# Capping the bytes of loads in flight at 1.25 MB in a two-layer decode kernel

## The chip, the cores and the metric

The kernel runs on one core of a Trainium2 chip. Its time is device time in microseconds (us), and lower is better. Runs of one kernel spread by about 1%; a run more than 1.5% above the fastest of its kernel counts as slow and is left out of the ratios (the medians quoted are of all runs). A ratio is the mean time of one kernel's fast runs over that of the other's of the same rounds on the same chip, so it is not quite the ratio of the medians quoted beside it.

The engines: TensorE (PE; its weight loads are PEld), VectorE (DVE), ScalarE (ACT), and SyncE (SP), which issues all DMA loads.

## The reference, cut to what matters

```python
def setup_inputs():                        # bfloat16 throughout
    x: (4, 1, 448)                         # 4 sequences ("tokens" below), one position each
    k_cache, v_cache: (4, 8, 8192, 256)    # 8 KV heads, 16 query heads
    wq: (448, 4096); wo: (4096, 448); w_gate, w_up: (448, 1792); w_down: (1792, 448)

x = x + A(layernorm(x))     # attention over the last 2048 positions of the cache
x = x + B(layernorm(x))     # FFN: (silu(x @ w_gate) * (x @ w_up)) @ w_down
x = x + A(layernorm(x))     # layer 2: the same weights and the same caches
x = x + B(layernorm(x))
```

There are 4 tokens x 8 heads x 2 layers = 64 "pairs" of one token with one KV head. A pair needs 1 MB of K and 1 MB of V; 16 pairs of the second layer find theirs still in SBUF. Everything loaded is 112.85 MB. (Sizes of loads and caps count 1 MB as 2^20 bytes, so 1.25 MB is 1.31 million bytes; totals, bytes in flight as measured, and rates count in millions.)

## The kernel before

The kernel builds a graph of operations, runs its own list scheduler over it, and emits each engine's instructions in the order planned, with the semaphore waits that the dependencies need. SyncE is an engine in this plan too: a load may be planned as soon as its destination is free, and nothing limits how many are queued.

```python
def dma(self, rank, nbytes, emit, sem, r=(), w=()):
    o = self.op(SP, 0.05, rank, emit, r=r, w=w)
    ...
def schedule(self):
    rate = 400e3
    ...
        t, e = best                      # earliest engine that has something ready
        o = min((o for o in avail[e] if ready_at[o] <= t + 1e-9), key=lambda o: (o.rank, o.i))
        o.start = t
        free[e] = t + o.dur
        if o.nbytes:
            chan = max(chan, t + 0.6) + o.nbytes / rate
            o.end = chan + 1.3           # planned landing
...
NK = 2; NKT = 5; NV = 6                  # buffers: raw K, transposed K, V
load(kvh + 0.6, 458752, wo_sb[...], ...)             # output projection, a piece per head
load(7.2, 3 * 458752, wg_sb[...], ...)               # FFN weights, whole
load(7.3, 1605632, wd_sb[...], ...)
...
for pos, (t, layer, kvh) in enumerate(seq):          # 64 pairs
    # K: two loads of 512 KB into a raw buffer; VectorE transposes each half (line KT)
    # V: four loads of 256 KB
    # TensorE: S = scores, M = maximum, P and Y = probabilities times V, A = output projection
```

A load is planned when its buffer is free. The weights' buffers are free from the start, so the plan puts V for six pairs, as many as there are buffers, and all output-projection and FFN loads ahead of the third pair's K, whose raw buffer waits for a transpose.

## Time and profile before

| | before |
|---|---|
| time, median (range) | 408.95 us (406.32 to 409.17, 3 runs) |
| TensorE, VectorE busy | 63%, 50% of the span |
| loads: share of 16 engines, mean rate | 76.6%, 280 GB/s |
| first FFN starts; second q projection starts | 109.3 us; 122.6 us |

From the page of the kernel before: busy tenths and the rate of the loads in 40 slices of 10.2 us each, the load queue's share, the chain that ended last, and the loads (count, KB each, median us from issue to landing):

```profile
PE   2155006638647656688778575887874778578965
...
DMA  7999999987970899973974999939849949745300
GB/s 304 386 387 382 399 396 398 395 269 232 397 266 14 265 392 395 396 270 116 378 278 152 385 399 395 354 110 336 300 161 322 395 157 340 259 142 185 101 2 3
...
q1 hardware_dynamic: 49184, 112.85, 76.6%
...
PE 40%; DVE 17%; DMA 15%; SPq 13%; issue 10%; ACT 4%; DVEq 0%
DMA Kr<-in_A_k_cache_dram 15%; DVE KT L528 11%; PE S L544 9%; PE Y L592 8%; SPq L536 7%; PE Z L437 6%; SPq L312 5%; PE A L611 5%; PE Z L399 3%; PE Z L456 3%; ACT oT L601 2%; DVE negm L560 1%; ACT qb L421 1%; PE Z L342 1%; PE Z L344 1%
...
Kr<-in_A_k_cache_dram SPq DMA_DIRECT2D x96, 512.0 KB, 7.6
V<-in_A_v_cache_dram SPq DMA_DIRECT2D x192, 256.0 KB, 8.1
```

In slices 2 to 8 the loads run at 382 to 399 GB/s, yet TensorE is busy at most six tenths of a slice and not at all in slices 5 and 6: it is starved although the load queue is full, because the wrong things are loaded. Later the loads pause again and again (14, 116, 110 GB/s). A load lands some 8 us after its issue: there is a long queue in front of it. (Z is the tile of the q projection and the FFN; the names of lines and tiles are the kernel's.)

SyncE's timeline of the kernel before (start, length, line and tiles, count), and TensorE's longest waits there (total us, times, longest):

```profile
35.96 2.77 SPq L312 DMA_DIRECT2D wg_sb<-in_B_w_gate_dram  x2
38.78 2.79 SPq L312 DMA_DIRECT2D wu_sb<-in_B_w_up_dram  x2
41.62 0.43 SPq L312 DMA_DIRECT2D wd_sb<-in_B_w_down_dram  x1
42.09 9.07 SPq L312 DMA_DIRECT2D wo_sb<-in_A_wo_dram  x1
51.21 2.84 SPq L522 DMA_DIRECT2D Kr<-in_A_k_cache_dram  x4
```

```profile
PE S L544 <- DVE KT L528: 31.8, 9, 22.4
...
PE S L565 <- DVE negm L560: 17.9, 9, 6.6
...
PE S L544 <- issue: 11.2, 9, 2.2
PE Y L592 <- issue: 9.2, 6, 2.7
PE Z L456 <- issue: 6.3, 4, 2.6
```

The third pair's K is issued at 51.2 us, behind all the weights. TensorE waits 22.4 us for its transpose. "Issue" is time in which TensorE waited for nothing that the profile shows; summed over its lines it is 36 us. The trace holds 60 transfers of 16,384 bytes on a queue called instruction, and all 17 "issue" waits of 1 us or more begin between 0.3 us before and 1.4 us after the start of one of them. So I call these waits instruction waits below; the name is a reading of that coincidence.

### The profile page before, as it was taken

The page shows a single profiled execution, that of the slowest core. Times are in us where ns is not written, and L with a number is a line of the kernel's source. Part 1 is how long each engine was busy: PE and PEld are TensorE (multiplying, and loading weights), DVE is VectorE, ACT ScalarE, POOL GpSimd, SP SyncE. Part 2 cuts the span into 40 slices and gives each one's busy share as a digit, 9 for nine tenths or more (in the row PEclk, how much of TensorE's full clock was granted, in tenths as well). Part 3 has the DMA queues.
Part 4 walks back from the last instruction along what each step waited for, and adds up shares of the span by engine and source line. Part 5 has one row for each costly group of instructions (what it writes and reads, how often), then busy time and mean ns, then how long its engine had stood idle before and what let it go on. Part 6 is the DMA issues. An engine that isn't in the chain of part 4 may idle for free.

```text
span 406.4 us, 16676 instructions
## 1 busy us (share of the span) xinstructions
PE 254.8 (63%) x7572; PEld 230.5 (57%) x7572; DVE 203.1 (50%) x642; ACT 58.6 (14%) x302; POOL 2.7 (1%) x11
## 2 busy tenths in 40 slices
PE   2155006638647656688778575887874778578965
PEld 2154005537646645577677465776763768467854
DVE  6721026668523554556537554746355365546432
ACT  1014001102101111111112111110121211011210
POOL 2000000000000000000000000000000000000000
DMA  7999999987970899973974999939849949745300
GB/s 304 386 387 382 399 396 398 395 269 232 397 266 14 265 392 395 396 270 116 378 278 152 385 399 395 354 110 336 300 161 322 395 157 340 259 142 185 101 2 3
DMA packets 49255, 113.91 MB, mean 280 GB/s; under 512 B 4889, under 2 KB 11041, under 8 KB 48801
## 3 DMA queue, kind: packets, MB, share of 16 engines
q1 hardware_dynamic: 49184, 112.85, 76.6%
q8 instruction: 60, 0.98, 1.0%
q14 instruction: 11, 0.08, 0.1%
HBM read 112.82 MB, written 0.00 MB: 278 GB/s over the span
## 4 chain that ended last, share of the span: by engine, by line
PE 40%; DVE 17%; DMA 15%; SPq 13%; issue 10%; ACT 4%; DVEq 0%
DMA Kr<-in_A_k_cache_dram 15%; DVE KT L528 11%; PE S L544 9%; PE Y L592 8%; SPq L536 7%; PE Z L437 6%; SPq L312 5%; PE A L611 5%; PE Z L399 3%; PE Z L456 3%; ACT oT L601 2%; DVE negm L560 1%; ACT qb L421 1%; PE Z L342 1%; PE Z L344 1%
## 5 line engine op out<-in xcount | busy, mean ns | idle before, releaser
L528 DVE STREAM_TRANSPOSE KT<-Kr 128x1024 uint32<-128x1024 uint32 x96 | 118.3, 1235 | 50.2 <-DMA Kr<-in_A_k_cache_dram 50.1
L544 PE MATMUL S<-qb,KT 128*128 128x8 bf16 x2048 | 65.0, 168 | 49.7 <-DVE KT L528 31.8
L544 PEld LDWEIGHTS S<-qb,KT 128*128 128x128 bf16 x2048 | 61.0, 105 | 53.6 <-DVE KT L528 33.3
L592 PE MATMUL Y<-pT,V 128*128 128x2 bf16 x2048 | 63.9, 165 | 14.3 <-issue 9.2
L592 PEld LDWEIGHTS Y<-pT,V 128*128 128x128 bf16 x2048 | 59.8, 104 | 16.5 <-issue 9.8
L611 PE MATMUL A<-oT,wo_sb 128*128 128x1 bf16 x1024 | 37.4, 166 | 17.6 <-ACT oT L601 12.5
L611 PEld LDWEIGHTS A<-oT,wo_sb 128*128 128x128 bf16 x1024 | 32.9, 105 | 25.4 <-ACT oT L601 19.5
L601 ACT ACTIVATE oT<-Y,rinv 128x2 bf16<-128x2 f32 x128 | 26.5, 258 | 112.9 <-PE S L565 50.9
L550 DVE TENSOR_REDUCE pmax<-S 128x2 bf16<-128x32 f32 x64 | 11.8, 184 | 48.2 <-PE S L544 46.4
L560 DVE TENSOR_REDUCE negm<-M 128x2 bf16<-128x256 f32 x64 | 26.1, 407 | 12.3 <-PE M L557 11.3
L569 ACT ACTIVATE praw<-S 128x32 bf16<-128x32 f32 x64 | 12.6, 196 | 99.8 <-PE S L565 99.8
L437 PE MATMUL Z<-xn,wu_sb 128*128 128x1 bf16 x336 | 24.1, 165 | 2.0 <-issue 2.0
L437 PE MATMUL Z<-xn,wg_sb 128*128 128x1 bf16 x336 | 24.1, 165 | 1.4 <-DVE xe L381 1.4
L565 PE MATMUL S<-negm,identb 128*128 128x32 bf16 x64 | 12.3, 192 | 19.5 <-DVE negm L560 17.9
L581 DVE TENSOR_REDUCE rs<-Y 128x2 f32<-128x32 f32 x64 | 11.3, 178 | 19.3 <-PE P L576 13.6
L557 PE MATMUL M<-identb,pmax 128*128 128x128 bf16 x64 | 20.1, 314 | 0.0
L437 PE MATMUL Z<-xe,wu_sb 128*128 128x1 bf16 x112 | 18.5, 165 | 1.7 <-issue 1.7
L565 PEld LDWEIGHTS S<-negm,identb 128*128 128x128 bf16 x64 | 6.9, 108 | 21.7 <-DVE negm L560 21.5
L437 PE MATMUL Z<-xe,wg_sb 128*128 128x1 bf16 x112 | 18.5, 165 | 1.1 <-issue 1.1
L437 PEld LDWEIGHTS Z<-xn,wu_sb 128*128 128x128 bf16 x336 | 17.7, 104 | 2.2 <-issue 2.1
L437 PEld LDWEIGHTS Z<-xn,wg_sb 128*128 128x128 bf16 x336 | 17.6, 104 | 1.8 <-DVE xe L381 1.8
L555 PE MATMUL M<-identb,pmax 128*128 128x128 bf16 x64 | 17.4, 272 | 1.8 <-DVE pmax L550 1.8
(70 smaller groups left out, 313.0 us busy)
## 6 DMA issues: line engine op xcount, KB each, us to landing
Kr<-in_A_k_cache_dram SPq DMA_DIRECT2D x96, 512.0 KB, 7.6
V<-in_A_v_cache_dram SPq DMA_DIRECT2D x192, 256.0 KB, 8.1
wo_sb<-in_A_wo_dram SPq DMA_DIRECT2D x8, 448.0 KB, 9.5
wq_sb<-in_A_wq_dram SPq DMA_DIRECT2D x3, 1024.0 KB, 6.9
wd_sb<-in_B_w_down_dram SPq DMA_DIRECT2D x1, 1568.0 KB, 14.6
wg_sb<-in_B_w_gate_dram SPq DMA_DIRECT2D x1, 1344.0 KB, 11.5
wu_sb<-in_B_w_up_dram SPq DMA_DIRECT2D x1, 1344.0 KB, 12.6
wq_sb<-in_A_wq_dram SPq DMA_DIRECT2D x1, 512.0 KB, 9.7
```

The lines of the kernel that those rows point to most:

```text
L312: return e.dma_start(dst, src)
L437: last = e.matmul(Zb[:, 32 * gi + fc:32 * gi + fc + 1], lhsT=lhsT, rhs=rhs, start=(n == 0), stop=(n == 111), skip_group_check=True)
L528: return e.transpose(dst[:, 2 * hf:2 * hf + 2], src[:, 2 * hf:2 * hf + 2])
L536: g.dma(pos + 0.3, 1 << 18, lambda e, vs=vs, vsrc=vsrc, a=a: e.dma_start(Vs[vs][:, a, :, :], vsrc[:, a, :, :]), f"v{vs}_{a}", w=(f"v{vs}_{ ...
L544: last = e.matmul(Sb[p_][:, 8 * gg:8 * gg + 8], lhsT=kt[:, gg, ce // 2, ce % 2, :], rhs=qb[t][:, kvh, ce, :, :], start=(gg == 0 and ce == ...
L555: e.matmul(Mb[:, 0:128], lhsT=pmax[p_][:, 0:1].broadcast_to([128, 128]), rhs=identb[:, :], start=True, stop=False, skip_group_check=True)
L557: return e.matmul(Mb[:, 128:256], lhsT=pmax[p_][:, 1:2].broadcast_to([128, 128]), rhs=identb[:, :], start=False, stop=True, skip_group_che ...
L560: g.op(DVE, 0.4, pos, lambda e, p_=p_: e.tensor_reduce(negm[p_][:, :], Mb[:, 0:256].rearrange("p (n k) -> p n k", n=2), AX.X, ALU.max, neg ...
L565: return e.matmul(Sb[p_][:, 0:32], lhsT=identb[:, :], rhs=negm[p_][:, :].unsqueeze(1).broadcast_to([128, 16, 2]), start=False, stop=True, ...
L592: last = e.matmul(Yb[p_][:, 2 * dh:2 * dh + 2], lhsT=Vs[vs][:, a, gg, 128 * dh:128 * dh + 128], rhs=pT[p_][:, k, :], start=False, stop=(dh ...
L601: last = e.activation(oT[p_][:, n, :], Yb[p_][:, 0:4].rearrange("p (d n) -> p n d", n=2)[:, n, :], ACT.Copy, scale=rinv[p_][:, n:n + 1])
L611: last = e.matmul(Ab[:, 4 * t + cc:4 * t + cc + 1], lhsT=wo_sb[:, 4 * kvh + k, c0:c0 + 128], rhs=oT[p_][:, k // 2, k % 2:k % 2 + 1], start ...
```

## The change

Its intent: issue loads in the order of need, and never queue much more than the memory needs to stay busy. SyncE waits, before each load, for the landing of an earlier one such that at most 1.25 MB (5 x 256 KB) is in flight, the new load included. The plan knows it, so the planned order shifts as well. The FFN weights are cut into pieces that fit.

```diff
+INFLIGHT = 5 << 18
...
+    @staticmethod
+    def _gate(issued, o):
+        if o.rank < 0:
+            return None
+        total = o.nbytes
+        for d in reversed(issued):
+            total += d.nbytes
+            if total > INFLIGHT:
+                return d
+        return None
...
             avail[e].remove(o)
+            if o.nbytes:
+                o.gate = self._gate(order[SP], o)
+                if o.gate is not None:
+                    t = max(t, o.gate.end)          # in the plan
             o.start = t
...
-            for d in sorted(o.deps, key=lambda d: -d.end):
-                if o.deps[d] and not has(k, d):
+            deps = dict(o.deps)
+            if o.nbytes and o.gate is not None:
+                deps[o.gate] = True                 # the wait itself
+            for d in sorted(deps, key=lambda d: -d.end):
+                if deps[d] and not has(k, d):
...
-            load(7.2, 3 * 458752, wsb[:, 0:3 * FF]..., nm + "a")
+            for cc in range(3):
+                load(7.2, 458752, wsb[:, cc * FF:cc * FF + FF], src[128 * cc:128 * cc + 128, :], f"{nm}{cc}")
...
-        load(7.3, 1605632, wd_sb[:, :, :], ..., "wd")
+        for i, k0 in enumerate((0, 4, 8, 12)):
+            k1 = min(k0 + 4, NFC)
+            load(7.3, (k1 - k0) * 114688, wd_sb[:, k0:k1, :], wd_v[:, k0:k1, :], f"wd{i}")
```

So there are three parts: a new order, the waits (the cap), and the pieces.

More of the change, by code (lines that the diff above doesn't have):

```diff
@@ L40 @@
     __slots__ = ("i", "eng", "dur", "rank", "emit", "deps", "succ", "nbytes", "dsem", "dval",
-                 "start", "end", "pos", "waits", "inc", "val", "known")
+                 "start", "end", "pos", "waits", "inc", "val", "known", "gate")
     def __init__(self, i, eng, dur, rank, emit):
@@ L323, in build @@
         for nm, wsb, src in (("wg", wg_sb, B_w_gate), ("wu", wu_sb, B_w_up)):
-            load(7.2, 3 * 458752, wsb[:, 0:3 * FF].rearrange("p (c n) -> p c n", c=3),
-                 src[0:384, :].rearrange("(c p) n -> p c n", p=128), nm + "a")
-            load(7.2, 229376, wsb[:, 3 * FF:], src[384:448, :].rearrange("r (h n) -> (r h) n", h=2), nm + "b")
-        load(7.3, 1605632, wd_sb[:, :, :], B_w_down.rearrange("(k p) n -> p k n", p=128), "wd")
+            for cc in range(3):
+                load(7.2, 458752, wsb[:, cc * FF:cc * FF + FF], src[128 * cc:128 * cc + 128, :], f"{nm}{cc}")
+            load(7.2, 229376, wsb[:, 3 * FF:], src[384:448, :].rearrange("r (h n) -> (r h) n", h=2), nm + "3")
+        wd_v = B_w_down.rearrange("(k p) n -> p k n", p=128)
+        for i, k0 in enumerate((0, 4, 8, 12)):
+            k1 = min(k0 + 4, NFC)
+            load(7.3, (k1 - k0) * 114688, wd_sb[:, k0:k1, :], wd_v[:, k0:k1, :], f"wd{i}")
         def small(t, rank, emit, r, w, dur=0.14, bank=()):
@@ L440, in gu @@
                 return last
-            g.op(PE, 3.4, rank, gu, r=(f"xn{t}", f"xe{t}", "wga", "wgb", "wua", "wub"), w=("z",), bank=("Z",))
+            g.op(PE, 3.4, rank, gu, r=(f"xn{t}", f"xe{t}", *(f"{n}{c}" for n in ("wg", "wu") for c in range(4))), w=("z",), bank=("Z",))
             g.op(SCA, 0.25, rank, lambda e: e.activation(th[:, :], Zb[:, 0:NFC], ACT.Tanh, scale=0.5), r=("z",), w=("th",),
@@ L459, in down @@
                 return last
-            g.op(PE, 1.8, rank, down, r=("hT", "wd"), w=("z",), bank=("Z",))
+            g.op(PE, 1.8, rank, down, r=("hT", "wd0", "wd1", "wd2", "wd3"), w=("z",), bank=("Z",))
             small(t, rank, lambda e: e.tensor_tensor(xs[:, t, 0, :], xs[:, t, 0, :], Zb[:, 64:68], op=ALU.add),
```

## The prediction

> **What bounds it now.** Not one engine. The page gives TensorE 63% of 406.4 us, VectorE 50%, the load queue 77%. The chain of waits: TensorE 40%, VectorE 17%, the K loads 15%, SyncE's issuing 13%, "issue" (TensorE waiting for nothing shown) 10%. By stages (windows): from 10 to 80 us the loads run at 382 to 399 GB/s while TensorE idles. SyncE's timeline shows why: after the first two K pairs it issues every V, output-projection and FFN weight load, and the third pair's K only at 51.2 us; its data land at 58.7. TensorE waits 22.4 us there for the transpose. FFN 1 starts at 109.3 us, the second q projection at 122.6. Afterwards a period of 16 pairs takes 83 to 87 us and moves some 25 MB (63 us at 397 GB/s); loads stand idle around each q projection (2 GB/s from 120 to 130 us) because buffers are full.
>
> **Removed.**
> 1. The wrong load order. The order listing of the changed kernel has K before V, pair by pair, FFN weights just before pair 7's V. TensorE follows the stream from about 20 us on. FFN 1 needs fewer S groups ahead of it (10 instead of 12).
> 2. Instruction starvation. TensorE's waits named "issue" sum to 36 us (27 waits, up to 2.7 us). The trace has 60 instruction transfers of 16 KB (the Trainium skill, "Runtime: NRT & Kernel Launch", Terms, gives 16 KiB refills). Stalls of 1.4 to 2.7 us fall where 7 to 14 loads are in flight, under 0.8 mostly where 3 or fewer are. The skill's "DMA: Bandwidth & Descriptors", Queues, rings and completion order, says rings are served in turn per packet, which would make depth harmless; the trace suggests otherwise. I expect about half of it back.
>
> **Added.** A waiting SyncE. A lone 512 KB K load takes 3.56 us from issue to landing, a lone 256 KB V 2.75; at 0.66 us per 256 KB that leaves a fixed 2.1 us. With 1.25 MB in flight I work out 5.8 us per fresh pair (2 MB) instead of 5.3; 7.4 with an output-projection piece instead of 6.4; the FFN weights, two 448 KB pieces in flight, 17 us instead of 12. [...]
>
> **On the critical path.** Start: FFN 1 near 98 us, second q projection 112 to 118 instead of 122.6: minus 5 to 10. Later periods: TensorE gains 4 to 5 us of issue stalls each and 3 to 5 us from K no longer queued behind V bursts (7.75 us K landings at 136.7 and 99.4). Against that, 12 fresh pairs at 5.8 us plus some 1 us of instruction hits each are about 80 us, close to the period itself, so the loads become a second, nearly equal limit and part of the gain is lost in imperfect overlap.
>
> Predicted 399 us, range 378 to 425. Chances: faster by over 2% 0.50, within 2% 0.28, slower 0.22.
>
> **What would show it.** K third pair landing near 25 us, not 58.7; the 22.4 us TensorE wait gone; median K landing 3.5 to 4.5 us instead of 7.6; GB/s of 300 to 350 in the first 90 us instead of 395; "issue" on TensorE at 12 to 22 us instead of 36; SyncE waiting mostly for loads; less full idleness of the queue at q projections.
>
> **What would make it wrong.** If instruction transfers halt the shallow stream for 2 us or more each, or the fixed latency under load is nearer 2.6 us, loads run below 300 GB/s and bound everything: 420 to 435 us. If the issue stalls vanish altogether and buffers hide the slower stream, 375 to 385.

## The result, and the profile after

The changed kernel takes 461.49 us (460.91 to 462.42, 4 runs) against 407.63 us (4 runs): ratio 1.132, 95% interval 1.126 to 1.138. It is clearly slower, far outside the predicted range.

The same parts of the page for the changed kernel (slices of 11.5 us):

```profile
PE   2243532401456735638757835557677487667874
...
DMA  7987877878786987887778777887797787877300
GB/s 313 333 245 274 258 262 239 261 229 259 261 285 221 280 281 258 282 263 250 250 257 267 258 255 259 261 282 243 273 292 265 264 282 239 297 267 235 117 3 2
...
q1 hardware_dynamic: 49296, 112.85, 74.3%
...
DMA 68%; PE 18%; DVE 7%; issue 3%; ACT 2%; SPq 1%; DVEq 0%
DMA V<-in_A_v_cache_dram 32%; DMA Kr<-in_A_k_cache_dram 25%; DMA wo_sb<-in_A_wo_dram 7%; PE S L568 4%; PE Y L616 4%; DVE KT L552 4%; PE A L635 2%; DMA wu_sb<-in_B_w_up_dram 2%; PE Z L461 2%; PE Z L423 2%; PE Z L480 1%; ACT oT L625 1%; DMA wg_sb<-in_B_w_gate_dram 1%; DMA wd_sb<-in_B_w_down_dram 1%; ACT qb L445 1%
...
Kr<-in_A_k_cache_dram SPq DMA_DIRECT2D x96, 512.0 KB, 5.1
V<-in_A_v_cache_dram SPq DMA_DIRECT2D x192, 256.0 KB, 4.2
```

The pauses are gone, and so is the rate: from the third slice to the 37th it is 221 to 297 GB/s, never 390. The same bytes are moved by engines that are busy 74.3% of a longer span. DMA makes up 68% of the chain that ended last; it was 15% before. A K load lands 5.1 us and a V load 4.2 us after its issue, instead of 7.6 and 8.1, but so few are in flight that this caps the rate.

SyncE's waits in the changed kernel, and TensorE's:

```profile
SPq L560 <- DMA Kr<-in_A_k_cache_dram: 129.6, 80, 10.3
SPq L546 <- DMA V<-in_A_v_cache_dram: 54.3, 57, 2.4
...
SPq L208 <- DMA V<-in_A_v_cache_dram: 26.0, 32, 2.7
```

```profile
PE Y L616 <- DMA V<-in_A_v_cache_dram: 37.7, 8, 19.9
PE S L589 <- DVE negm L584: 28.2, 14, 7.1
...
PE S L568 <- DVE KT L552: 17.6, 4, 5.7
PE Y L616 <- issue: 16.3, 8, 4.2
```

SyncE now waits for the loads themselves. (L546 issues K, L560 V; L208 is the line that emits waits.) The order did what it was meant to: SyncE's timeline has the third pair's K issued at 21.0 us, and the 22.4 us wait for a transpose is gone. But TensorE waits 19.9 us once for the V behind the FFN weights.

```profile
15.55 2.90 SPq L560 DMA_DIRECT2D V<-in_A_v_cache_dram  x4
18.93 0.38 SPq L333 DMA_DIRECT2D wo_sb<-in_A_wo_dram  x1
21.00 2.79 SPq L546 DMA_DIRECT2D Kr<-in_A_k_cache_dram  x2
23.84 5.59 SPq L560 DMA_DIRECT2D V<-in_A_v_cache_dram  x4
```

Reading the latency against the window: from 15 us on, the trace has 1.19 MB in flight on average, and a load (weighted by bytes) lands after 4.62 us. 1.19 MB / 4.62 us = 258 GB/s, the measured rate, as it must be: the three figures are bound to each other by arithmetic, so this is no evidence of a cause. The question is where the 4.6 us come from, and whether order or waits cost the time.

### The profile page after: what moved, and what is told of

Its sections match the earlier page's. It is cut to its first block, busy times and chain, and to the rows that moved or that the text cites. A ratio compares the mean times of both kernels' runs of the same rounds, so it can differ in the third digit from the quotient of the medians.

```text
span 459.1 us, 16738 instructions
## 1 busy us (share of the span) xinstructions
PE 254.4 (55%) x7572; PEld 229.8 (50%) x7572; DVE 204.0 (44%) x642; ACT 59.0 (13%) x302; POOL 2.7 (1%) x11
## 3 DMA queue, kind: packets, MB, share of 16 engines
q1 hardware_dynamic: 49296, 112.85, 74.3%
## 4 chain that ended last, share of the span: by engine, by line
DMA 68%; PE 18%; DVE 7%; issue 3%; ACT 2%; SPq 1%; DVEq 0%
DMA V<-in_A_v_cache_dram 32%; DMA Kr<-in_A_k_cache_dram 25%; DMA wo_sb<-in_A_wo_dram 7%; PE S L568 4%; PE Y L616 4%; DVE KT L552 4%; PE A L635 2%; DMA wu_sb<-in_B_w_up_dram 2%; PE Z L461 2%; PE Z L423 2%; PE Z L480 1%; ACT oT L625 1%; DMA wg_sb<-in_B_w_gate_dram 1%; DMA wd_sb<-in_B_w_down_dram 1%; ACT qb L445 1%
## 5 line engine op out<-in xcount | busy, mean ns | idle before, releaser
L568 PE MATMUL S<-qb,KT 128*128 128x8 bf16 x2048 | 63.9, 168 | 34.3 <-DVE KT L552 17.6
L635 PEld LDWEIGHTS A<-oT,wo_sb 128*128 128x128 bf16 x1024 | 33.9, 106 | 19.8 <-ACT oT L625 19.1
L574 DVE TENSOR_REDUCE pmax<-S 128x2 bf16<-128x32 f32 x64 | 11.6, 182 | 45.2 <-PE S L568 45.1
L593 ACT ACTIVATE praw<-S 128x32 bf16<-128x32 f32 x64 | 12.6, 197 | 83.0 <-PE S L589 82.8
L423 PE MATMUL Z<-xn,wq_sb 128*128 128x1 bf16 (+1 forms) x480 | 17.7, 165 | 1.3 <-DVE xe L405 1.3
```

Source lines behind the costliest of these rows:

```text
L423: last = e.matmul(o, lhsT=lhsT, rhs=rhs, start=(hh == 0 and ee == 0 and cc == 0), stop=(hh == 15 and ee == 1 and cc == 3), skip_group_chec ...
L568: last = e.matmul(Sb[p_][:, 8 * gg:8 * gg + 8], lhsT=kt[:, gg, ce // 2, ce % 2, :], rhs=qb[t][:, kvh, ce, :, :], start=(gg == 0 and ce == ...
L593: g.op(SCA, 0.35, pos, lambda e, p_=p_: e.activation(praw[p_][:, :], Sb[p_][:, 0:32], ACT.Exp, scale=1.0 / 16.0), r=(f"s{p_}",), w=(f"praw ...
L635: last = e.matmul(Ab[:, 4 * t + cc:4 * t + cc + 1], lhsT=wo_sb[:, 4 * kvh + k, c0:c0 + 128], rhs=oT[p_][:, k // 2, k % 2:k % 2 + 1], start ...
```

## The experiments

All variants below are the changed kernel with the constant split in two, so that plan and waits can be capped separately:

```diff
-INFLIGHT = 5 << 18
+SCHED_INFLIGHT = 5 << 18     # what the plan, and so the order, assumes; None: no cap
+WAIT_INFLIGHT = 10 << 18     # what SyncE really waits for; None: no waits
-    def _gate(issued, o):
-        if o.rank < 0:
+    def _gate(issued, o, limit):
+        if limit is None or o.rank < 0:
...
-                o.gate = self._gate(order[SP], o)
-                if o.gate is not None:
-                    t = max(t, o.gate.end)
+                g = self._gate(order[SP], o, SCHED_INFLIGHT)
+                if g is not None:
+                    t = max(t, g.end)
+                o.gate = self._gate(order[SP], o, WAIT_INFLIGHT)
```

With the plan's value at 5 << 18, all instructions stand in the changed kernel's order on every engine; with None they stand in the order of before, save for the FFN pieces. The waits are not needed for correctness, so leaving them out is free of races.

Theory A: the waits cap the rate, because a load takes some 4.5 us to land. Theory B: the new order itself makes the loads slow.

### Order alone, waits alone, pieces alone, and 2.5 MB

The order alone: `WAIT_INFLIGHT = None`.

> The changed kernel's instruction order on every engine, none of its waits for earlier loads. Theory A (the waits cap the loads: with several loads in flight one takes some 4.5 us to land, and 1.25 MB in 4.5 us is no more than 290 GB/s): loads back at 390 GB/s in the busy stretches, time 380 to 405 us, that is at or below before. Theory B (the new order itself makes the loads slow): 435 to 460 us with 250 to 300 GB/s.

Measured: 399.92 us (4 runs), ratio 0.976 (0.969 to 0.984). Faster, though the interval does not clear 2%. I read the profile of its repeat, `new_order_free_b` below; its rate is back at 373 to 403 GB/s in slices 2 to 10:

```profile
GB/s 301 384 399 390 399 390 403 386 397 373 256 304 256 399 398 378 235 186 319 194 162 327 395 398 379 165 220 352 262 159 375 316 184 360 197 156 192 91 2 3
```

The waits alone: `SCHED_INFLIGHT = None`, `WAIT_INFLIGHT = 5 << 18`.

> The order of before (with the FFN weights in pieces), and each load held back to 1.25 MB in flight. Theory A: loads at 240 to 270 GB/s through the first 100 us and in every later busy stretch, 450 to 480 us. Theory B: near before, 405 to 425 us.

Measured: 473.50 us, ratio 1.160 (1.152 to 1.168). The old order at the same cap has the changed kernel's low rate:

```profile
GB/s 320 331 301 281 239 243 249 249 262 234 227 252 240 178 256 236 267 251 267 225 247 255 247 250 256 268 287 246 248 272 250 238 269 243 240 277 250 143 3 1
```

The pieces alone: both None.

> Only the FFN weights in 448 KB pieces, no waits, the order of before. Both theories: within 1% of before (404 to 412 us). If the pieces alone cost, over 415 us.

Measured: 408.33 us, ratio 1.002 (0.997 to 1.007). The pieces cost nothing.

The new order with twice the window: `WAIT_INFLIGHT = 10 << 18`.

> The changed kernel's order with 2.5 MB in flight instead of 1.25. Theory A: latency grows to some 6.5 us by the queue alone, the loads run at 350 to 390 GB/s, time 385 to 415 us. Theory B: no change, 435 to 460 us. A third theory (a fixed cost of each wait of SyncE, whatever the depth): 440 to 460 us as well, since the number of waits is much the same.

Measured: 393.94 us, ratio 0.965 (0.958 to 0.971). Faster than before. Theory A holds in all four runs; B fails in the three where it forecast something else (for the pieces both said the same); the third theory, a fixed cost of each wait, falls too: this program waits for landings about as often (258 such waits in its listing against 247 in the changed kernel's), and the loss is gone. The rate of this run, and its K and V landings:

```profile
GB/s 305 383 399 391 397 387 401 386 396 399 307 283 288 400 368 358 267 234 335 170 174 350 396 393 398 181 250 307 204 214 369 277 224 392 177 138 176 83 2 2
...
Kr<-in_A_k_cache_dram SPq DMA_DIRECT2D x96, 512.0 KB, 6.5
V<-in_A_v_cache_dram SPq DMA_DIRECT2D x192, 256.0 KB, 6.2
```

It runs at 383 to 401 GB/s through slices 2 to 10, with landings of 6.5 and 6.2 us.

### How deep must it be, and do coarse loads waste the window

`WAIT_INFLIGHT = 7 << 18`:

> The changed kernel's order with 1.75 MB in flight. If the rate is simply the bytes in flight over the landing time (1.19 MB over 4.6 us is the 258 GB/s of the changed kernel; at 1.7 MB I expect some 5.2 us), the loads run at about 325 GB/s and the time is 405 to 425 us. If there is a threshold and not a slope, it is within 1% of 2.5 MB (390 to 398 us) or of 1.25 MB (456 to 466 us).

Measured: 427.67 us, ratio 1.041 (1.033 to 1.049). A slope, not a threshold, and a little worse than I expected: from 15 us on the profiled run has 1.57 MB in flight and 5.57 us per load, so 281 GB/s over the stretch (which also contains pauses).

`WAIT_INFLIGHT = 14 << 18`:

> The changed kernel's order with 3.5 MB in flight. If 2.5 MB is already enough to keep the loads at their full rate and a deeper queue only lengthens TensorE's waits for instructions (42 us at 2.5 MB, 52 us with no cap), 394 to 400 us, with instruction waits between those two. If 2.5 MB still costs rate, 385 to 392 us.

Measured: 398.84 us, ratio 0.972 (0.966 to 0.979). TensorE's instruction waits were 44.7 us in the profiled run. The interval overlaps that of 2.5 MB: above 2.5 MB no further gain was seen.

K in loads of 256 KB at 1.25 MB (each transpose now waits for two of them, a line left out here):

```diff
-                for hf in range(2):
+                for qq in range(4):
...
-                        return e.dma_start(Kr[kr][:, 2048 * hf:2048 * hf + 2048], ...)
-                    g.dma(pos - 1.2, 1 << 19, kload, f"k{kr}_{hf}", w=(f"kr{kr}_{hf}",))
+                        return e.dma_start(Kr[kr][:, 1024 * qq:1024 * qq + 1024], ...)
+                    g.dma(pos - 1.2, 1 << 18, kload, f"k{kr}_{qq}", w=(f"kr{kr}_{qq}",))
```

> The changed kernel at 1.25 MB with each 512 KB K load cut into two of 256 KB, so that five equal loads can be in flight. If coarse pieces waste the window (the mean in flight is 1.19 MB of 1.31), it fills and a load lands sooner: 425 to 450 us. If only the bytes in flight count and these were nearly full already: 450 to 465 us.

Measured: 447.79 us, ratio 1.091 (1.086 to 1.097). Finer loads take back about a third of the loss (1.132 to 1.091) but no more.

The changed kernel with its one constant at 2.5 MB, `INFLIGHT = 10 << 18`:

> The changed kernel with its one constant at 2.5 MB, in the scheduler's plan too, so that the order shifts a little. If the plan's order matters less than the cap: 388 to 400 us, near the 394 us of the fixed order with 2.5 MB. If the order drifts back to that of before: 400 to 408 us.

Measured: 397.29 us, ratio 0.970 (0.966 to 0.975). One constant would have turned the change into a gain.

### Do order and cap add up, and is the cap worth anything

The order of before with 2.5 MB:

> The order of before (FFN weights in pieces), held to 2.5 MB in flight. If order and cap add up (order 0.976 of before, 2.5 MB on top of it 0.988): 400 to 408 us. If a cap helps only where the order is right, since it lets less run ahead of need: 408 to 420 us.

Measured: 402.65 us, ratio 0.986 (0.980 to 0.992).

The best version again, and the uncapped one, five rounds each on one chip:

> The best version so far again, to tell it from the uncapped one on the same chip: 0.960 to 0.970 of before, 390 to 397 us, TensorE's waits for instructions 40 to 44 us.

> The changed order without any cap again: 0.970 to 0.985 of before, TensorE's waits for instructions 48 to 54 us. If the cap of 2.5 MB is worth anything, this is slower than it by 0.5% or more; if not, the two intervals overlap widely.

Measured: 393.79 us, ratio 0.962 (0.955 to 0.968), with the cap; 399.74 us, ratio 0.976 (0.970 to 0.982), without. The intervals do not touch, so 2.5 MB is worth something. But TensorE's instruction waits were 42.6 against 45.2 us in these profiled runs: 2.6 us of the 6, from one profile each. My explanation of that gain, fewer instruction waits, could therefore be at most a part of it and is not shown; its cause stays open. The three-cornered comparison, as ratios to before:

| waits | order of before | new order |
|---|---|---|
| 1.25 MB | 1.160 | 1.132 |
| 1.75 MB | | 1.041 |
| 2.5 MB | 0.986 | 0.965, 0.962 |
| 3.5 MB | | 0.972 |
| none | 1.002 | 0.976, 0.976 |

The new order is worth about 2.4% at each depth where both were run (1.132 / 1.160 = 0.976; 0.962 / 0.986 = 0.976). The cap multiplies on top, and 1.25 MB costs 16%.

K in 256 KB loads at 2.5 MB:

> 2.5 MB in flight with K loads of 256 KB. At 1.25 MB the finer loads recovered a third of the loss; at 2.5 MB the loads already run near their full rate, so 388 to 398 us, within 1% of the version with 512 KB loads. If more loads in the queue cost SyncE or the engines: 398 to 405 us.

Measured: 399.58 us, ratio 0.980 (0.975 to 0.985): slower than with 512 KB loads (0.962), and outside the 388 to 398 us that I expected: it lies in the range written down for the case that more loads in the queue cost something. What they cost was not looked into. At this depth finer loads do not help.

### Are the 4.6 us the loads' own?

The prediction named two risks in one sentence: instruction transfers beside the loads, and a longer fixed latency under load. These runs issue the same loads in the same order with the same cap, and compute nothing (so a buffer's next load waits only for its last one, not for its reader). Their outputs are wrong, which doesn't matter for the times.

```diff
+    def loads_only(self, eng, dsems):
+        before = {}
+        for o in self.order[SP]:
+            if o.dsem.startswith("o"):
+                continue
+            for d in (o.gate, before.get(o.dsem)):        # the cap; the last load of this buffer
+                if d is not None and d.dsem[0] != "o":
+                    eng.wait_ge(dsems[d.dsem], d.dval)
+            o.emit(eng).then_inc(dsems[o.dsem], 16)
+            before[o.dsem] = o
...
-        @block.tensor ... @block.vector ... @block.scalar ... @block.gpsimd ...
```

> Wrong result on purpose: SyncE's loads of the changed kernel in the same order with the same holding back to 1.25 MB, and no compute at all (each buffer's next load waits only for its last one). If the 4.6 us of a load is the loads' own, the stream runs at 250 to 280 GB/s as in the changed kernel and 113 MB take 410 to 450 us. If it comes from what computes beside them (instruction transfers, VectorE in the same memory), 330 to 375 GB/s, the rate that my prediction worked out from lone loads, and 310 to 350 us.

> The same with 2.5 MB. Loads' own: 370 to 395 GB/s, 290 to 310 us. Interference: 390 to 400 GB/s, 285 to 292 us.

> The same with no cap but the buffers' (some 4 MB): 390 to 400 GB/s, 283 to 292 us, under every theory; it is the rate to compare with.

> 1.25 MB again, with K in 256 KB loads and no compute. If uneven, coarse loads are what keeps the rate down, 290 GB/s or more, clearly above the run with 512 KB loads; if the landing time of whatever is in flight is fixed, within 5% of it.

Measured, one run each: 422.41, 295.68, 294.35 and 406.70 us. The loads held to 1.25 MB take longer alone than the whole kernel before (407.04 us on that chip). From the pages of the 1.25 MB and the uncapped run, rate in 40 slices, the load queue's share, and landings:

```profile
GB/s 307 342 267 248 246 273 254 270 242 250 263 296 292 247 262 246 257 285 252 274 269 255 269 294 287 299 294 279 287 242 265 279 289 226 293 242 280 262 299 158
...
q1 hardware_dynamic: 49296, 112.85, 81.8%
...
Kr<-in_A_k_cache_dram SPq DMA_DIRECT2D x96, 512.0 KB, 5.0
V<-in_A_v_cache_dram SPq DMA_DIRECT2D x192, 256.0 KB, 4.0
```

```profile
GB/s 260 376 406 398 393 395 394 394 401 392 394 396 397 400 395 401 396 396 401 395 401 397 397 399 401 395 398 396 399 402 395 400 394 399 399 399 400 394 395 93
...
q1 hardware_dynamic: 49296, 112.85, 101.3%
...
Kr<-in_A_k_cache_dram SPq DMA_DIRECT2D x96, 512.0 KB, 10.5
V<-in_A_v_cache_dram SPq DMA_DIRECT2D x192, 256.0 KB, 10.2
```

No instruction queue of TensorE is left to blame, and the rate is 226 to 299 GB/s from the third slice to the last but one all the same. With 2.5 MB it is 390 to 408 GB/s in nearly every slice, as without a cap. So most of the landing time is the loads' own: 4.50 us here against 4.62 us in the changed kernel. The run with 256 KB K loads was 3.7% shorter than the one with 512 KB, which is inside the 5% written down for a landing time that is fixed: a load took 4.55 us there, and the finer loads only filled the window better (1.27 against 1.21 MB in flight on average). Coarseness is a small part.

Where does the time sit? The load queue's packets took 81.8% of 420.6 us, that is 344 us of each engine on average, against 101.3% of 292.5 us, or 296 us (packets overlap a little). So of 128 us lost, about 48 are longer packets and the rest idle engines.

The idle part can be looked into through the loads' completions. The Trainium skill, "DMA: Bandwidth & Descriptors", Why a DMA increments its semaphore by 16 and not by 1, says that each of the up to 16 engines of a load finishes by itself and posts its own completion; only the full 16 mean that the data have landed. The page of the changed kernel counts 5,000 packets under 512 B, which is 312 loads x 16, plus 4 for the 4-row input and 4 for the outputs. These are four-byte writes, and they tell how unevenly the engines finish.

When a lone K load of before (issued at 363.59 us) ran, its first data moved 0.97 us after issue and its 16 writes fell between 366.05 and 366.87. With others in flight they lie further apart: by the semaphores' records, the first and the 16th completion of a load lie a median of 1.6 us apart in the changed kernel and 1.4 us in the 1.25 MB run without compute. In the changed kernel, when a load lands, a median of 5 completions of later loads are already there, and 12 to 26 when the second K load of the third to eighth pair lands, with three later loads (48 completions) in flight. So some engines have gone on to later loads while others still hold up the oldest one, and SyncE may not issue more until those are done; it loses no time of its own there, as it issues the next load 0.02 us (median) after the landing that it waits for. With 2.5 MB and no compute the spread is much the same, 1.5 us, and the rate is full: a deep queue would give the quick engines other work. That is a measurement of the unevenness; that it causes the idle share is inferred. A rival is not excluded: the time between issue and first data (0.97 us for the lone load), in which a part of the small window moves nothing. From lone loads, that time included, the prediction worked out 5.8 us per fresh pair, which is about 360 GB/s, so it can be a part of the loss but by that estimate not all of it. Why some engines lag under load, or their packets take longer, is left open.

### What the order gained, and where part of it went

TensorE's start of the second q projection and the pairs of K and V landed by then (from the traces):

| | second q projection | pairs landed | periods after it |
|---|---|---|---|
| before | 122.6 us | 14.5 | 86.6, 83.4, 62.2, tail 51.6 |
| new order, no cap | 105 us | 12.6 | 92, 86, 64, tail 51 |
| new order, 2.5 MB | 105 us | 12.8 | 87, 85, 63, tail 51 |
| changed kernel | 144.5 us | 12.2 | 103, 95, 64, tail 53 |

(Start times of the new order are whole microseconds; the spans of the profiled runs are 406.4, 398.2, 391.1 and 459.1 us.) The new order wins 18 us at the start, as hoped, yet ends only 8 us ahead without a cap. Before had nearly two more pairs, about 4 MB or 10 us at 397 GB/s, in store when it got there. A missing store would explain what is given back in the next period; but the run with 2.5 MB has the same store and lost nothing there (86.8 us; 90 us in the profile of its first run). So this too stays open.

## Why the prediction was wrong, point by point

- **The bound before and its cause: right.** The misplaced K at 51.2 us was the start's loss. The order alone brought the first FFN from 109 to 88 us and the second q projection from 122.6 to 105 us, more than the 112 to 118 forecast with the cap's cost in it. In the changed kernel itself, with the cap, they came at 123.5 us (forecast: near 98) and 144.5 us.
- **"that leaves a fixed 2.1 us": this is the step that failed.** I took it from loads issued into an idle queue (3.56 us for K, 2.75 for V; the Trainium skill, "DMA: Bandwidth & Descriptors", Anatomy of one DMA, gives about 2 us plus size over rate for a DMA issued from GpSimd, a path that this kernel does not use; an estimate from its figures is 3.2 and 2.6 us, close to these) and used it for loads with others in flight. With 1.2 MB in flight a load took 4.62 us; the prediction's own subtraction, from the medians of 5.1 and 4.2 us, leaves 3.8 us for K and 3.5 for V instead of 2.1. So a fresh pair works out at 8.1 us (2.1 MB at 258 GB/s), not 5.8; a pair with an output-projection piece 9.8 us (the first K loads of the third to eighth pair land at 25.6 to 74.7 us, five steps), not 7.4; the FFN weights 23 us (85.0 to 107.9), not 17. The mechanism was named, its size was too small by 2.3 us per fresh pair.
- The trace of before pointed to it. The second K load after an idle queue took 4.6 to 5.5 us six times (132.0, 218.4, 301.8, 330.7, 352.2, 365.4 us), and half-microsecond bins with 1.0 to 1.5 MB in flight moved about 270 GB/s on average, with 2.5 to 3 MB about 360, from 3 MB on about 390. I had put the low value down to the start of bursts.
- **"the loads become a second, nearly equal limit": wrong in size.** They became the limit nearly alone: 68% of the chain, against 18% for TensorE.
- **"If instruction transfers halt the shallow stream for 2 us or more each, or the fixed latency under load is nearer 2.6 us": the second half came true, beyond its size; the first was the wrong culprit.** Without any instruction transfers a load still took 4.50 us instead of 4.62, and the stream was no better than 268 GB/s. The number in that fallback, below 300 GB/s, came true; its time, 420 to 435 us, did not: the last load landed at 432.4 us, and a tail of 27 us came on top.
- **"I expect about half of it back": the number was right, its reason is not shown, and it was worth nothing.** "Issue" fell from 36 to 22 us. With the cap it rises with depth in both orders (new: 21.7, 33.4, 41.9, 44.7 us for 1.25, 1.75, 2.5 and 3.5 MB; old: 9.4 us for 1.25 MB, 32.8 for 2.5 MB, 37.1 without a cap). But in the shallow kernels TensorE was waiting for data anyway.
- **The signs given.** K of the third pair near 25 us: right (25.6). The 22.4 us wait gone: right. Median K landing of 3.5 to 4.5 us: no (5.1). "Issue" at 12 to 22 us: right (21.7), with the doubt just named. 300 to 350 GB/s in the first 90 us: no, 239 to 274 after the second slice. SyncE waiting mostly for loads: right.

## What to carry to other kernels

A cap on bytes in flight must be set from the landing time of loads under load, not of a lone one: divide the window by it and compare with the full rate. Here 1.25 MB gave two thirds of the rate and 2.5 MB nearly all of it, so in this kernel issuing in order of need wants a cap of about twice the first figure, or none. And when a change bundles an order with a wait, run each alone: here one was worth 2.4% and the other cost 16%.

The best version run: the new order with `WAIT_INFLIGHT = 10 << 18`, 0.962 of before (393.79 us).

## What the Trainium skill lacked or had wrong

- "DMA: Bandwidth & Descriptors", Bandwidth and Rules for kernel authors, speaks of the size of one DMA (at least 1 MiB for the best rate) and not of the bytes in flight. Here loads of 256 and 512 KB ran at some 397 GB/s once 2.5 MB was in flight (384 over that run's whole span), and at 268 GB/s over the span with 1.25 MB; it was depth that counted.
- The same page, Anatomy of one DMA, tells the cost of one DMA, for those issued from GpSimd, and no landing time with others in flight. Here a 512 KB load into an idle queue took 3.56 us; with about 1.2 MB in flight, and nothing computing, loads took 4.5 us, where 1.25 MB at the full rate of 397 GB/s is 3.3 us.
- No page gives a figure for how far apart the 16 engines of one load finish: with nothing computing, a median of 1.4 us with 1.25 MB in flight and 1.5 us with 2.5 MB.
- The same page, Queues, rings and completion order, has the engines serve their rings in turn, packet by packet. TensorE's waits for nothing that the profile shows grew with the cap, from 21.7 us at 1.25 MB to 44.7 us at 3.5 MB in the new order and from 9.4 us at 1.25 MB to 32.8 us at 2.5 MB in the old. Whether that is the queue's depth or TensorE being starved less was not separated. The refills of 16 KiB of "Runtime: NRT & Kernel Launch", Terms, do appear (59 or 60 transfers of 16,384 bytes).
